# The last output tile of a transformer layer computed and stored in two column groups of 448 and 128

## Chip, cores, metric

One core of one Trainium2 chip runs the whole kernel. The metric is the device time of one execution in microseconds. It contains about 1.7 us that lie outside the profiled span (the profiled execution of the kernel before took 406.61 us with a span of 404.9).

One more length is used throughout, the **tail**: from the start of the first matmul of the last W2 tile to the end of the span. It is read from the records of a trace. The **flight** of a store is the time from the start of its issue to its landing. The **granted clock** is the share of full speed that TensorE was given.

## The reference

An attention block with a learned feature map, then a GELU MLP, both with residuals, over 2048 rows of 576 columns. Only the end matters here:

```python
def _B_ref(x, w1, b1, w2, b2):                    # D = 576, F = 4608
    y = _layernorm(x, axis=-1)
    h = _gelu(jnp.einsum("bsd,df->bsf", y, w1) + b1)
    return jnp.einsum("bsf,fd->bsd", h, w2) + b2
...
h2 = h + _B_ref(_layernorm(h, axis=-1), ...)      # 2048 x 576, bf16: the output
```

## The kernel before

The MLP runs in 8 rounds of 256 rows. Each round computes the hidden activations (W1 and GELU) and then two tiles of 128 rows x 576 output columns (W2). A tile needs 36 steps over the 4608 hidden values; the kernel lays its accumulator out in banks of 512 columns, so every step is one matmul of 512 columns and one of 64, each with its own weight load. The 64-column matmuls run five steps behind.

```python
def w2_tile(r, j, slots):
    mb = (3, 2)[j]
    for i in range(NF + LAG):                     # NF = 36, LAG = 5
        ...
        for (m, bk, o, n) in ((i, mb, 0, 512), (i - LAG, TAILB, 512, 64)):
            if 0 <= m < NF:
                P.add("pe", ... e.matmul(ps_all[:, 512*bk:512*bk + n], w2_lhs(m, j), w2_rhs(m, o, n),
                                         start=(m == 0), stop=(m == NF - 1)) ...)
    t = RT * r + j
    ob = t % 2
    P.add("pool", ... tmpo = x_all[:, t, :] + b2bc ...)          # residual + bias
    for bk, o, n in ((TAILB, 512, 64), (mb, 0, 512))[::1 - 2 * j]:
        P.add("dve", ... ostage[ob][:, o:o + n] = ps_all[bank bk] + tmpo[:, o:o + n] ...,
              writes=[res(f"ostage{ob}")] ...)
    P.dma(ch_out[ob], lambda e: e.dma_start(outr[t * 128:(t + 1) * 128, :], ostage[ob][:, :]),
          reads=[res(f"ostage{ob}")])
...
P.commit()
P.final_dma_waits("sp")     # SyncE waits for every DMA channel that it has not yet waited for
```

(`...` marks cuts; the bodies of the operations are shortened to what they compute.) `P.add` and `P.dma` record an operation; the waits between engines follow from the resources and banks that it names. A "channel" is a semaphore of its own for a row of DMAs.

The softmax here doesn't subtract the row's maximum and nothing guards it: scores larger than these inputs give would overflow.

Of the kernel before, what the change touches and what calls it, by code (L numbers as in the profile page):

```python
# [6 lines left out]
ALU = mybir.AluOpType  # L7
# [231 lines left out]
def bass_sequential_preLN__linear_kernel_hedgehog__mixer_channel_mlp__prompt_kernel(  # L239
    nc: bass.Bass,  # L240
    A_x: bass.AP,
    A_wqkv: bass.AP,
    A_w_phi: bass.AP,
    A_wo: bass.AP,
    B_x: bass.AP,
    B_w1: bass.AP,
    B_b1: bass.AP,
    B_w2: bass.AP,
    B_b2: bass.AP,
    out: bass.AP,  # L250
):
    _build(nc, A_x, A_wqkv, A_w_phi, A_wo, B_w1, B_b1, B_w2, B_b2, out)
# [48 lines left out]
def _build(nc, A_x, A_wqkv, A_w_phi, A_wo, B_w1, B_b1, B_w2, B_b2, out):  # L301
# [5 lines left out]
    NF = F // 128  # L307
    NT = S // 128
    RT = 2
    NR = NT // RT  # L310
# [6 lines left out]
    outr = out[0]  # L317

    P = Prog(nc)
# [3 lines left out]
    def sb(name, shape, dtype=BF16):  # L323
        return ctx.enter_context(nc.sbuf_tensor(name, shape, dtype))
# [4 lines left out]
    x_all = sb("x_all", [128, NT, D])  # L329
# [7 lines left out]
    ostage = [WQ[:, D * i:D * i + D] for i in range(2)]  # L337
# [32 lines left out]
    b2bc = sb("b2bc", [128, D])  # L370
# [12 lines left out]
    tmpo = sb("tmpo", [128, D], F32)  # L383
    maskf = tmpo[:, 0:133].rearrange("p (g d) -> p g d", g=7)

    ps_all = ctx.enter_context(nc.psum_tensor("ps_all", [128, 4096], F32))
    PR = 4096
    bank = [Bank() for _ in range(8)]
# [3 lines left out]
    def res(name):  # L392
        if name not in R:
            R[name] = Res(name)
        return R[name]

    def rr(fmt, n):
        return [res(fmt.format(i)) for i in range(n)]
# [6 lines left out]
          reads=[res("ident")], writes=[res("ident")])  # L405
# [3 lines left out]
          reads=[res("maskf")], writes=[res("maskf")])  # L409
    P.add("pool", lambda e: e.affine_select(maskf[:, :, :], maskf[:, :, :], pattern=[[18, 7], [0, 19]],  # L410
                                            compare_op=ALU.is_ge, fill=0.0, base=17, channel_multiplier=-1),
          reads=[res("maskf")], writes=[res("maskf")])
    P.add("pool", lambda e: e.tensor_copy(mask7[:, :, :], maskf[:, :, :]),
          reads=[res("maskf"), res("tmpo")], writes=[res("mask7")])
# [48 lines left out]
    for c in (0, 2):  # L463
# [9 lines left out]
          writes=[res("s2_0"), res("table")])  # L473
# [163 lines left out]
    for k, (b0, b1, nr) in enumerate(((0, 3, 126), (3, 4, 72), (4, 5, 126))):  # L637
# [5 lines left out]
            reads=[WPH[k], res("mask7")], writes=[res(f"phib{k}")])  # L643
# [10 lines left out]
    for g in range(4):  # L654
        n = 7 if g < 3 else 4
        P.add("pool", lambda e, g=g, n=n: e.tensor_copy(mask25[:, 7 * g:7 * g + n, :], mask7[:, 0:n, :]),
              reads=[res("mask7")], writes=[res("mask25")])
    P.add("pool", lambda e: e.tensor_copy(
        kvr[:, :, 0:25, 19:20], mask25[:, :, 0:1].unsqueeze(1).to_broadcast([128, 2, 25, 1])),
        reads=[res("mask25")], writes=[res("kvr1")])  # L660
    P.add("pool", lambda e: e.tensor_copy(
        kvr[:, :, 25:32, 19:20], mask7[:, :, 0:1].unsqueeze(1).to_broadcast([128, 2, 7, 1])),
        reads=[res("mask7")], writes=[res("kvr1")])
# [268 lines left out]
    def attn_N(t, bset):  # L932
        attn_N_mm(t, bset)
        attn_N_copy(bset, 0)
        attn_N_small(0)
        attn_N_inv(0)
        attn_N_mul(t, bset, 0, "pool")
# [11 lines left out]
    def wo_half(t, bset, step):  # L949

        A, C, B = bset
        ob = t % 2

        def one(lane, k, h, c, first, last):
            bk = (A, C)[k]
            o = 0 if c == 4 else DHF * k
            P.add(lane, lambda e: e.matmul(  # L957
                ps_all[:, 512 * bk:512 * bk + DHF], oT[ob][h:h + 64, c, :], wo_sb[h:h + 64, c, o:o + DHF],
                start=first, stop=last, skip_group_check=True),
                reads=[res(f"oT{ob}"), res("wo"), res("wo4")], banks=[bank[bk]])  # L960

        cs = (4, 0, 1, 2, 3) if step == 0 else (0, 1, 2, 3)
        lo = [lambda c=c: one("pe0", step, 0, c, c == 4, step == 1 and c == 3) for c in cs]
        hi = [lambda c=c: one("pe8", 1 - step, 64, c, c == 4, step == 1 and c == 3) for c in cs]
        return lo, hi
# [105 lines left out]
    for s in range(2):  # L1071
# [3 lines left out]
            reads=[res("mask25")], writes=[res(f"kvra{s}")], banks=[bank[5 + s]])  # L1075
# [4 lines left out]
        reads=[res("mask7")], writes=[res("kvrb")], banks=[bank[7]])  # L1080
# [4 lines left out]
    for m0 in range(0, NW2B, 8):  # L1085
# [31 lines left out]
          reads=[res("neghalf")] + rr("Eq{}", NR), writes=[res("sums0")])  # L1117
# [12 lines left out]
    TAILB = 4  # L1130
    LAG = 5
    ch_out = [P.chan(f"out{i}", "sp") for i in range(2)]
# [38 lines left out]
    def w1_round(r, extra):  # L1171

        lo, hi = [], []
        for s in range(NF // 2):
            k = s % 3
            u8 = s + (2, -1, -1)[k]
            lo += [(f, None) for f in w1_half(r, s, 0, k < 2)]
            hi += [(f, None) for f in w1_half(r, u8, 64, k == 0)]
            if k == 1:
                hi.append((None, lambda s=s: w1_act(r, s - 1)))  # L1180
            if k == 2:
                hi.append((None, lambda s=s: (w1_act(r, s), w1_act(r, s - 1))))
            for fl, fh, after in extra.get(s, ()):
                lo += [(f, None) for f in fl]
                hi += [(f, None) for f in fh]
                if after:
                    hi.append((None, after))
        hi = [(None, None)] * SKEW + hi
        n8 = 0
        while lo or n8 < len(hi):  # L1190
            if lo:
                f = lo.pop(0)[0]
                f()
            while n8 < len(hi):
                f, g = hi[n8]
                if f is None and g is not None:
                    g()
                    n8 += 1
                    continue
                if f is not None:  # L1200
                    f()
                n8 += 1
                break
            while n8 < len(hi) and hi[n8][1] is not None:
                hi[n8][1]()
                n8 += 1

    def w2_lhs(m, j):
        return hmid[:, m, 128 * j:128 * j + 128]

    def w2_rhs(m, o, n):
        return w2a[:, m, o:o + n] if m < NW2A else w2b[:, m - NW2A, o:o + n]

    def w2_tile(r, j, slots):
        mb = (3, 2)[j]
        for i in range(NF + LAG):
            if i in slots:
                slots[i]()
            for (m, bk, o, n) in ((i, mb, 0, 512), (i - LAG, TAILB, 512, 64)):
                if 0 <= m < NF:  # L1220
                    P.add("pe", lambda e, m=m, bk=bk, o=o, n=n: e.matmul(  # L1221
                        ps_all[:, 512 * bk:512 * bk + n], w2_lhs(m, j), w2_rhs(m, o, n),
                        start=(m == 0), stop=(m == NF - 1)),
                        reads=[res(f"hm{m}_{j}"), res(f"w2_{m}")], banks=[bank[bk]])
        t = RT * r + j
        ob = t % 2
        P.add("pool", lambda e: e.tensor_tensor(tmpo[:, :], x_all[:, t, :], b2bc[:, :], ALU.add),  # L1227
              reads=[res("b2"), res(f"x{t}")], writes=[res("tmpo"), res("maskf")])
        for bk, o, n in ((TAILB, 512, 64), (mb, 0, 512))[::1 - 2 * j]:
            P.add("dve", lambda e, bk=bk, o=o, n=n: e.tensor_tensor(  # L1230
                ostage[ob][:, o:o + n], ps_all[:, 512 * bk:512 * bk + n], tmpo[:, o:o + n], ALU.add),
                reads=[res("tmpo")], writes=[res(f"ostage{ob}")] + (R_weffq if t < 2 else []), banks=[bank[bk]])
        P.dma(ch_out[ob], lambda e: e.dma_start(outr[t * 128:(t + 1) * 128, :], ostage[ob][:, :]),
              reads=[res(f"ostage{ob}")])

    for r in range(NR):
        a, b = RT * (r + 1), RT * (r + 1) + 1
        extra, slots = {}, ({}, {})
        if r + 1 < NR:
            ia, ib = (3, 12) if r else (9, 16)  # L1240
            for t, i in ((a, ia), (b, ib)):
                extra[i] = [(*wo_half(t, S1, 0), None)]
                extra[i + 1] = [(*wo_half(t, S1, 1), lambda t=t: attn_wo(t, S1))]
            if r == 0:
                extra[3] = [((), (), lambda: attn_N(b, S1))]
        if r + 2 < NR:
            slots[0][2] = lambda: attn_N(a + RT, S1)
            slots[1][6] = lambda: attn_N(b + RT, S1)
        w1_round(r, extra)
        w2_tile(r, 0, slots[0])  # L1250
        w2_tile(r, 1, slots[1])

    P.commit()
    P.final_dma_waits("sp")
# [32 lines left out]
```

## Time and profile before

| | before |
|---|---|
| time, median of 3 (lowest to highest) | 406.77 us (406.11 to 407.04) |
| span of the profiled execution | 404.9 us, granted clock 1.0 |
| TensorE busy | 97% of the span |
| tail | 12.245 us: 8.98 of matmuls, 3.26 after them |

TensorE, busy for 97% of the span, bounds the kernel from beginning to end. The tail is the one place where other engines stand in the open: after the last matmul come two adds, one store and the waits for it. The prediction shows the lines. One more view, the busy time of each engine before, in and after the last tile (columns: stretch, its length, busy time and count of each engine, granted clock, DMA share, GB/s), shows the handover: 8.95 us of TensorE in 9.00, then 0.01 in 3.40.

```profile
392.60:401.60 9.00, 8.95 (x78) 4.61 (x75) 0.91 (x2) 0.00 (x0) 1.27 (x1) 1.00 0.05 16
401.60:405.00 3.40, 0.01 (x1) 0.00 (x0) 0.91 (x2) 0.00 (x0) 0.00 (x0) 1.00 0.12 43
```

### The profile page before, as it was taken

The numbers are of one execution on the slowest core, as the hardware profiler recorded it, in microseconds if no ns is written. First come the engines' busy times: TensorE is split into PE (matmuls) and PEld (weight loads), VectorE is DVE, ScalarE is ACT, GpSimd is POOL, SyncE is SP. The second block draws the span as 40 slices with busy tenths as digits, with TensorE's granted clock in tenths as the row PEclk, the third lists the DMA queues.
The fourth block names the chain that finished last, engine by engine and source line by source line (L and its number), as shares of the span: only waits on it lengthen the run. The fifth ranks groups of instructions, "written<-read, shape, count | busy, mean of one in ns | idle before, by whom it ended". The sixth has DMA issues, their size and how long they took to land.

```text
span 404.9 us, 11594 instructions
## 1 busy us (share of the span) xinstructions
PE 393.9 (97%) x4958; PEld 289.6 (72%) x4999; DVE 176.7 (44%) x415; ACT 184.8 (46%) x429; POOL 91.6 (23%) x130
## 2 busy tenths in 40 slices
PE   7899999999999999999999999999999999999996
PEld 5566666868955995599569856985797579659953
DVE  6999998876254323422442333243225402300000
ACT  6898955678820472057006600750264027404800
POOL 4759640112114002200220022002200220111000
PEclk9999999999999999999999999999999999999999
DMA  9587488981101101101111011001100110000000
GB/s 259 98 124 178 125 168 258 314 287 19 35 18 38 27 19 33 32 18 19 35 36 29 18 32 31 19 19 32 33 19 18 31 32 19 19 15 18 2 2 29
DMA packets 45594, 25.86 MB, mean 64 GB/s; under 512 B 32744, under 2 KB 44520, under 8 KB 45544
## 3 DMA queue, kind: packets, MB, share of 16 engines
q1 hardware_dynamic: 44784, 24.97, 24.5%
q8 instruction: 39, 0.64, 0.7%
q10 hardware_dynamic: 760, 0.17, 0.3%
q14 instruction: 11, 0.09, 0.1%
HBM read 15.13 MB, written 2.36 MB: 43 GB/s over the span
## 4 chain that ended last, share of the span: by engine, by line
PE 87%; ACT 6%; DVE 4%; issue 1%; DMA 1%; POOL 0%; ACTq 0%; DVEq 0%
PE ps_all L1221 34%; PE ps_all L1153 33%; PE ps_all L957 4%; PE ps_all L745 4%; PE ps_all L835 3%; PE ps_all L762 3%; PE ps_all L857 2%; PE ps_all L804 2%; ACT RA L1164 1%; ACT RB L752 1%; ACT Eq L841 1%; DMA x_all<-in_A_x_dram 1%; DVE RB L786 1%; DVE sums L773 1%; DVE x_all L979 1%
## 5 line engine op out<-in xcount | busy, mean ns | idle before, releaser
L1164 ACT ACTIVATE RA<-ps_all,b1T 128x256 bf16<-128x256 f32 x288 | 115.1, 479 | 176.6 <-PE ps_all L1153 161.9
L1153 PE MATMUL ps_all<-yT,w1sb 64*128 64x256 bf16 x2304 | 151.9, 269 | 0.0
L1153 PEld LDWEIGHTS ps_all<-yT,w1sb 64*128 64x128 bf16 x2304 | 136.2, 94 | 5.1
L1221 PE MATMUL ps_all<-w2a,RA 128*128 128x512 bf16 (+1 forms) x624 | 93.9, 284 | 2.0 <-ACT RA L1164 1.1
L1221 PEld LDWEIGHTS ps_all<-w2a,RA 128*128 128x128 bf16 x640 | 45.8, 98 | 35.7 <-ACT RA L1164 1.7
L1153 PE MATMUL ps_all<-yT,w1t 64*128 64x256 bf16 x288 | 70.9, 270 | 0.0
L1221 PE MATMUL ps_all<-RB,RA 128*128 128x512 bf16 (+1 forms) x498 | 66.6, 284 | 0.4
L1230 DVE TENSOR_TENSOR WQ<-ps_all,tmpo 128x64 bf16<-128x64 f32 (+1 forms) x32 | 14.6, 457 | 104.1 <-PE ps_all L1221 91.8
L1221 PEld LDWEIGHTS ps_all<-RB,RA 128*128 128x128 bf16 x512 | 33.4, 98 | 32.3
L979 DVE SCALAR_TENSOR_TENSOR x_all<-ps_all,x_all 128x576 bf16<-128x576 f32 x16 | 12.1, 758 | 82.8 <-PE ps_all L957 82.4
L1001 POOL TENSOR_TENSOR st<-st,neghalf 128x1 f32<-128x1 f32 x16 | 8.8, 552 | 136.3 <-DVE st L998 133.7
L925 POOL TENSOR_TENSOR obuf<-tpn 128x576 bf16<-128x576 f32 x14 | 19.6, 1400 | 84.0 <-DVE tpn L918 74.4
L841 ACT ACTIVATE Eq<-ps_all 128x512 bf16<-128x512 f32 (+1 forms) x48 | 25.1, 526 | 12.2 <-PE ps_all L835 11.3
L1227 POOL TENSOR_TENSOR tmpo<-x_all,b2bc 128x576 f32<-128x576 bf16 x16 | 20.4, 1273 | 43.2 <-DVE WQ L1230 43.2
L957 PE MATMUL ps_all<-wo_sb,OTR 64*128 64x288 bf16 x288 | 29.7, 283 | 0.5 <-ACT OTR L567 0.2
L1153 PEld LDWEIGHTS ps_all<-yT,w1t 64*128 64x128 bf16 x288 | 26.3, 94 | 1.9
L835 PE MATMUL ps_all<-yT,WQ 128*128 128x256 bf16 x200 | 25.2, 273 | 0.2 <-ACT Eq L841 0.2
L786 DVE TENSOR_TENSOR RB<-ps_all,RB 128x1152 bf16<-128x1152 f32 x16 | 21.6, 1352 | 3.4 <-PE ps_all L762 3.3
L957 PEld LDWEIGHTS ps_all<-wo_sb,OTR 64*128 64x128 bf16 x288 | 19.6, 94 | 3.8 <-PE ps_all L957 0.8
L762 PE MATMUL ps_all<-RB,yT 128*128 128x64 bf16 (+1 forms) x157 | 21.7, 284 | 0.2
L752 ACT ACTIVATE RB<-ps_all 128x576 bf16<-128x576 f32 x32 | 19.0, 648 | 5.8 <-PE ps_all L745 5.3
L745 PE MATMUL ps_all<-RA,yT 128*128 128x64 bf16 (+1 forms) x152 | 20.6, 281 | 1.1 <-ACT tpn L487 0.4
(104 smaller groups left out, 316.8 us busy)
## 6 DMA issues: line engine op xcount, KB each, us to landing
w1sb<-in_B_w_dram SPq DMA_DIRECT2D x8, 576.0 KB, 5.5
w2a<-in_B_w_dram SPq DMA_DIRECT2D x4, 720.0 KB, 7.4
RB<-in_B_w_dram SPq DMA_DIRECT2D x2, 1152.0 KB, 8.5
out_dram<-WQ SPq DMA_DIRECT2D x16, 144.0 KB, 1.8
x_all<-in_A_x_dram SPq DMA_DIRECT2D x3, 576.0 KB, 5.7
w2a<-in_A_wqkv_dram SPq DMA_DIRECT2D x2, 288.0 KB, 3.7
RB<-in_A_wqkv_dram SPq DMA_DIRECT2D x1, 576.0 KB, 5.8
w1t<-in_B_w_dram SPq DMA_DIRECT2D x2, 288.0 KB, 3.8
```

The costliest lines, as they stand in the source:

```text
L745: P.add("pe", lambda e, c=c, o=o, n=n: e.matmul(ps_all[:, 512 * KB + o:512 * KB + o + n], yT[:, c, sl * 128:(sl + 1) * 128], weffk[:, c, o ...
L752: P.add("act", lambda e, s=s: e.activation(Ek[eb][:, D * s:D * s + D], ps_all[:, 512 * KB:512 * KB + D], AF.Exp, scale=1.0 if s == 0 else ...
L762: P.add("pe", lambda e, c=c, o=o, n=n: e.matmul(ps_all[:, 512 * VB + o:512 * VB + o + n], yT[:, c, sl * 128:(sl + 1) * 128], wv[:, c, o:o ...
L786: P.add("dve", lambda e, s0=s0, s1=s1: e.tensor_tensor(vx(t)[:, s0:s1, :, 0:DH], ps_all[:, 512 * VB:512 * VB + D].rearrange("p (h d) -> p ...
L835: P.add("pe", lambda e, i=i, c=c, h0=h0: e.matmul(ps_all[:, 512 * bk + RW * i:512 * bk + RW * i + RW], weffq[:, c, DH * h0:DH * h0 + 128], ...
L841: P.add("act", lambda e, s=s: e.activation(Eq[:, r, s, bs[0]:bs[0] + n, :], ps_all[:, 512 * bk:512 * bk + RW * n].rearrange("p (b t) -> p ...
L925: P.add(oeng, lambda e: e.tensor_tensor(obuf[ob][:, 0:D], tpn[:, 0, :], tpn[:, 1, :], ALU.add), reads=[res("tpn")], writes=[res(f"obuf{ob}")])
L957: P.add(lane, lambda e: e.matmul(ps_all[:, 512 * bk:512 * bk + DHF], oT[ob][h:h + 64, c, :], wo_sb[h:h + 64, c, o:o + DHF], start=first, s ...
L1153: P.add(lane, lambda e: e.matmul(ps_all[:, o:o + RW], lhs, yT[h:h + 64, c, ys], start=first, stop=not begin and i == 1 and c == 3, skip_gr ...
L1164: P.add("act", lambda e, m=m, o=o: e.activation(hmid[:, m, :], ps_all[:, o:o + RW], AF.Gelu_apprx_tanh, bias=b1T[:, m:m + 1]), reads=[res( ...
L1221: P.add("pe", lambda e, m=m, bk=bk, o=o, n=n: e.matmul(ps_all[:, 512 * bk:512 * bk + n], w2_lhs(m, j), w2_rhs(m, o, n), start=(m == 0), st ...
L1227: P.add("pool", lambda e: e.tensor_tensor(tmpo[:, :], x_all[:, t, :], b2bc[:, :], ALU.add), reads=[res("b2"), res(f"x{t}")], writes=[res(" ...
```

## The change

The intent is to have most of the last tile summed, added and on its way to memory while TensorE still works on the rest. Only the 16th tile is touched: its 576 columns are split 448 + 128, each group runs through all 36 steps by itself, then is added, then stored: the first on output channel 0, the second on channel 1, the two that the earlier tiles use in turn.

```diff
+    def w2_last(r, j):
+        t, ob = RT * r + j, (RT * r + j) % 2
+        P.add("pool", lambda e: e.tensor_tensor(tmpo[:, :], x_all[:, t, :], b2bc[:, :], ALU.add), ...)
+        for k, (bk, o, n) in enumerate(((2, 0, 448), (TAILB, 448, 128))):
+            for m in range(NF):
+                P.add("pe", lambda e, m=m, bk=bk, o=o, n=n: e.matmul(
+                    ps_all[:, 512 * bk:512 * bk + n], w2_lhs(m, j), w2_rhs(m, o, n),
+                    start=(m == 0), stop=(m == NF - 1)), ...)
+            P.add("dve", lambda e, bk=bk, o=o, n=n: e.tensor_tensor(
+                ostage[ob][:, o:o + n], ps_all[:, 512 * bk:512 * bk + n], tmpo[:, o:o + n], ALU.add),
+                reads=[res("tmpo")], writes=[res(f"ostage{ob}{k}")] + ..., banks=[bank[bk]])
+            P.dma(ch_out[k], lambda e, o=o, n=n: e.dma_start(
+                outr[t * 128:(t + 1) * 128, o:o + n], ostage[ob][:, o:o + n]), reads=[res(f"ostage{ob}{k}")])
...
-        w2_tile(r, 1, slots[1])
+        if r + 1 < NR:
+            w2_tile(r, 1, slots[1])
+        else:
+            w2_last(r, 1)
```

More of the change, by code (lines that the diff above doesn't have):

```diff
@@ L1212, in w2_rhs @@
         return w2a[:, m, o:o + n] if m < NW2A else w2b[:, m - NW2A, o:o + n]
+    def w2_last(r, j):
+        t, ob = RT * r + j, (RT * r + j) % 2
+        P.add("pool", lambda e: e.tensor_tensor(tmpo[:, :], x_all[:, t, :], b2bc[:, :], ALU.add),
+              reads=[res("b2"), res(f"x{t}")], writes=[res("tmpo"), res("maskf")])
+        for k, (bk, o, n) in enumerate(((2, 0, 448), (TAILB, 448, 128))):
+            for m in range(NF):
+                P.add("pe", lambda e, m=m, bk=bk, o=o, n=n: e.matmul(
+                    ps_all[:, 512 * bk:512 * bk + n], w2_lhs(m, j), w2_rhs(m, o, n),
+                    start=(m == 0), stop=(m == NF - 1)),
+                    reads=[res(f"hm{m}_{j}"), res(f"w2_{m}")], banks=[bank[bk]])
+            P.add("dve", lambda e, bk=bk, o=o, n=n: e.tensor_tensor(
+                ostage[ob][:, o:o + n], ps_all[:, 512 * bk:512 * bk + n], tmpo[:, o:o + n], ALU.add),
+                reads=[res("tmpo")], writes=[res(f"ostage{ob}{k}")] + ([res(f"ostage{ob}")] if k == 0 else []), banks=[bank[bk]])
+            P.dma(ch_out[k], lambda e, o=o, n=n: e.dma_start(
+                outr[t * 128:(t + 1) * 128, o:o + n], ostage[ob][:, o:o + n]), reads=[res(f"ostage{ob}{k}")])
     def w2_tile(r, j, slots):
```

## The prediction

> **What bounds the kernel now.** I read the first page for the engine that is always busy, then the chain of work that ended last over the last 22 us, then the timeline of the last tile instruction by instruction, and last the queue of the sync engine, which issues the store and waits for it. On the page:
>
> ```profile
> PE 393.9 (97%) x4958; PEld 289.6 (72%) x4999; DVE 176.7 (44%) x415; ACT 184.8 (46%) x429; POOL 91.6 (23%) x130
> PE 87%; ACT 6%; DVE 4%; issue 1%; DMA 1%; POOL 0%; ACTq 0%; DVEq 0%
> ```
>
> TensorE is the bound from end to end, so a change in one tile of 16 can matter in two ways only: through the time that the tile keeps TensorE, and through what follows the last matmul, when nothing else is left to overlap. The diff touches nothing before the last W2 tile. The chain, at its end:
>
> ```profile
> 396.87 4.76 PE ps_all L1221 x42
> 401.63 0.00 issue
> 401.63 0.70 DVE WQ L1230
> 402.33 0.02 issue
> 402.35 0.22 DVE WQ L1230
> ```
>
> TensorE leads up to 401.63 us; then VectorE adds 512 columns (0.69 us) and 64 columns (0.22 us) one after the other, both in the open. What follows is the store: timeline, then the DMA view of the last 3 us, then the sync engine's waits.
>
> ```profile
> 402.65 0.33 SPq L1233 DMA_DIRECT2D out_dram<-WQ  x1
> ...
> out_dram<-WQ SPq DMA_DIRECT2D x1, 144.0 KB, 1.7
> ...
> SPq L226 <- DMA out_dram<-WQ: 0.2, 1, 0.2
> ```
>
> The store is issued at 402.65, lands 1.74 us later at 404.39 (both from the trace's record of this one DMA), and the program ends at 404.87. The third line is easy to pass over: of that flight SyncE waits only 0.2 us. The records of its queue say why. After issuing the store it works through some twenty waits for every earlier load, each about 60 ns apart, from 403.03 to 404.22, and only then comes to the store's own. So a store that lands faster gains at most about 0.17 us; from there the list is the bound.
>
> How the last tile feeds TensorE, from the timeline of that tile:
>
> ```profile
> 397.38 0.38 PE L1221 MATMUL ps_all<-RB,RA 128*128 128x512 bf16 x1
> 397.60 0.19 PE L1221 MATMUL ps_all<-w2a,RA 128*128 128x64 bf16 x1
> 397.63 0.38 PE L1221 MATMUL ps_all<-RB,RA 128*128 128x512 bf16 x1
> 397.85 0.19 PE L1221 MATMUL ps_all<-w2a,RA 128*128 128x64 bf16 x1
> 397.87 0.38 PE L1221 MATMUL ps_all<-RB,RA 128*128 128x512 bf16 x1
> ```
>
> Read the starts, not the durations, which overlap: 512 columns take 0.216 us and 64 take 0.029, 0.245 a pair, although each has its own weight load. The lag of five leaves five 64-column matmuls alone at the end (starts 401.303 to 401.420 us in the records, 29 ns apart, one bank), so repeated accumulation into one bank costs nothing extra, and a load can hide behind as little as 29 ns.
>
> [...] the trace of before does not bear it out. Its 128-column matmuls with a weight load each are the transposes (first line below), whose starts in the records are 56 ns apart (88.302, 88.358, 88.414, 88.470); and a group of eight 133-column and two 76-column matmuls (second line) takes 0.72 us in all[...].
>
> ```profile
> 88.30 0.39 PE L563 MATMUL ps_all<-ident,ybuf 128*128 128x128 bf16 x4
> 44.66 0.72 PE L804 MATMUL ps_all<-RB 128*128 128x133 bf16 x10
> ```
>
> [...] the two forms here show 691 and 224:
>
> ```profile
> L1230 DVE TENSOR_TENSOR WQ<-ps_all,tmpo 128x512 bf16<-128x512 f32 x16 | 11.1, 691 | 40.1 <-PE ps_all L1221 39.8
> L1230 DVE TENSOR_TENSOR WQ<-ps_all,tmpo 128x64 bf16<-128x64 f32 x16 | 3.6, 224 | 64.0 <-PE ps_all L1221 51.9 <-issue 8.6 <-POOL tmpo L1227 3.2
> ```
>
> [...] The new last store has rows of 256 bytes (128 columns of bf16), the old one 1152. No store of before is that narrow, so no line here shows its price. [...] of 1.74 us, the packets run from 403.48 to 404.01 only; 0.83 us pass before them and 0.38 after.
>
> **The change part by part.**
> Removed: the lagged pairing in tile 15 (36 matmuls of 512 and 36 of 64 columns), the adds of 512 and 64, one store of 144 KB. Added: 36 matmuls of 448, then 36 of 128, adds of 448 and 128, stores of 112 KB and 32 KB on the two output channels. The comparison of the queues shows no other difference: one more DMA on SyncE, equal counts on ACT and DVE, the same 72 matmuls. GpSimd's add of residual and bias waits for the same adds as before and is done some 6 us before it is needed (from 394.01 for 1.27 us).
> TensorE: before 36 x (215.8 + 29.2) = 8.82 us. [...] The same 576 columns a weight, the same 72 fixed costs: zero.
> The first group ends about 392.63 + 6.81 = 399.44. Its add (448 columns: 624 ns) and its store (issue 0.33, landing 1.7) are over by about 402.2, the issue by 400.9: all beside the second group's 2.01 us of matmuls or before the second store needs the queue.
> Last matmul: it starts at 392.63 + 8.82 - 0.06 = 401.39; a 128-column matmul lasts 219 ns by the transposes, so 401.61.
> Add of 128 columns: [...] It waits for one semaphore only; VectorE operations of this sort (the copies after the kv matmuls) start 37 ns after the matmul's modelled end. The old first add started 190 ns after its own last matmul, with two more waits of 50 ns ahead of it; those waits now stand before the 448-column add, out of sight. So 401.65 to 401.94, against 402.58 before: 0.64 us gained. It is 0.69 + 0.03 + 0.22 = 0.94 taken away and 0.29 put back, less 0.02 because the old add, freed by the 512-column group before the last 64-column matmuls were through, began 17 ns after TensorE's last end and the new one begins 37 ns after it.
> Store: issued 75 ns after the add as before, at 402.02. Its packets are 256 bytes: before, each engine ran eight rows 47 ns apart, 0.38 us. If a short row takes a third of that, landing comes 0.25 us earlier, 1.5 us after issue, at about 403.5. But the list of waits ends 1.62 us after the issue, at 403.64, against the old landing-bound check at 404.41. Gain at the end: 0.77 us. If the short rows save nothing, it is 0.64.
> I choose 0.72, between the two and nearer the list.
>
> **The rivals.**
> (a) Weight loads bind at 128 columns: [...] Against it: the 56 ns of the transposes and the 29 ns at the end of this very tile. I give it one in twenty.
> (b) The narrow store is slow. [...] Against it: there is only 32 KB, and most of the flight is before and after the packets. One in six.
> (c) The end is hidden anyway, behind the list of waits. It takes away at most the 0.1 us by which landing would beat it; it cannot take the 0.64, because the list starts with the issue of the last store and moves with it.
> (d) Run noise. Three runs of before span 0.93 us, more than the whole gain.
>
> **Range and chances.** The profiled execution of before took 406.61 with a span of 404.9, so about 1.7 us lie outside the span and do not move. 406.77 - 0.72 = 406.05. The median of before stands a little above the middle of its own runs, so I round down to 406.0. The range takes (b) at one end and a luckier set of runs at the other: 405.4 to 406.6. Two per cent is 8.1 us; nothing in the last tile (about 9 us of matmuls, 3 us of tail) could move that much: within 2% at 0.99.
>
> **What would show it.** Right: in the last 12 us the 128-column matmuls start 56 ns apart; the add of 128 columns takes 0.29 us and is the only VectorE piece of the chain after the last matmul; the 448-column add lies inside the matmuls; the last store issues at about 402.0, and the span is near 404.15. SyncE's wait for the last store should shrink from 0.2 us to almost nothing. Wrong: [...] landing over 1.8 us after issue (b); the 448-column add or its store delaying the second; or anything changed before 392 us, which the diff gives no reason for.

Passages that no trace or run of this case shows are cut from the prediction, and the cuts are marked. The sum stays as it was: 0.77 us gained at the end, 0.64 if the short rows save nothing, 0.72 chosen, 406.77 - 0.72 = 406.05, rounded down to 406.0. Terms are cut out of it: the matmuls of the two groups (6.81 and 2.01 us, together the 8.82 of before, hence zero for TensorE) and the working of the 128-column add (0.29 us). For these and for the 624 ns of the 448-column add an estimate from the trace of before gives the same: a straight line through its matmuls of 64 and 512 columns (29.2 and 215.8 ns) passes 55.9 at 128, with the transposes at 56 beside it, and 189.1 at 448, and leaves 2.5 ns at no columns (the "fixed cost" of each), and one through its adds of 64 and 512 columns (224 and 691 ns) passes 291 at 128 and 624 at 448. The "it" that the trace does not bear out is rival (a), a slower run of loads and matmuls. Of the group of ten matmuls only the reading is left: in the records the next matmul starts 0.560 us after the first of the ten, 1216 columns at 2.17 a ns. Rival (b) supposed, with nothing here to show it, that a narrow row takes twice the 47 ns: 0.38 us more, a gain of about 0.26, 406.5.

## The result

| | before | after |
|---|---|---|
| median of 4 runs (lowest to highest) | 406.9 us (406.11 to 407.19) | 406.0 us (405.57 to 406.78) |
| ratio, 95% interval | | 0.9983 [0.9962, 1.0004] |
| the same in a later, longer comparison (10 runs, 6 runs) | 407.0 us | 406.21 us, 0.9981 [0.9968, 0.9994] |
| tail, first trace / repeats | 12.245 / 12.249 us | 11.452 / 11.451, 11.448 us |

A ratio is the mean time of one kernel's fast runs over that of the other's of the same rounds, so not quite the ratio of the medians. By the first comparison alone the change could be nothing; the second leaves 1 outside its interval; the tails settle it: 0.80 us, repeated to 5 ns.

The chain of work that ended last, after (start, length, what; the columns of the chain in the prediction). The adds of 0.70 + 0.02 + 0.22 us at the end have become one of 0.29:

```profile
383.63 8.93 PE ps_all L1237 x72
392.56 8.84 PE ps_all L1220 x72
401.39 0.02 issue
401.42 0.29 DVE WQ L1224
```

TensorE and VectorE in the timeline after. The 448-column add (0.62 us) starts at 399.56, under the 128-column matmuls; twenty of these start at 399.20 and the next group of sixteen at 400.32, 56 ns for each:

```profile
399.20 1.28 PE L1220 MATMUL ps_all<-w2a,RA 128*128 128x128 bf16 x20
399.56 0.62 DVE L1224 TENSOR_TENSOR WQ<-ps_all,tmpo 128x448 bf16<-128x448 f32 x1 [5.86 <-PE ps_all L1220]
...
400.32 1.06 PE L1220 MATMUL ps_all<-RB,RA 128*128 128x128 bf16 x16
401.42 0.29 DVE L1224 TENSOR_TENSOR WQ<-ps_all,tmpo 128x128 bf16<-128x128 f32 x1 [1.23 <-PE ps_all L1220]
```

The stores after (bytes, median us from issue to landing), and what SyncE's queue waited for from 399 us on (total, times, longest):

```profile
out_dram<-WQ SPq DMA_DIRECT2D x1, 112.0 KB, 1.7
out_dram<-WQ SPq DMA_DIRECT2D x1, 32.0 KB, 1.5
...
SPq L226 <- DVE WQ L1224: 7.2, 2, 6.1
SPq L1275 <- PEq L1275: 0.2, 1, 0.2
```

The last of these lines belongs to the program's own end. The line "SPq L226 <- DMA out_dram<-WQ", 0.2 us before, is gone: when SyncE comes to its last wait, at 403.38 us, the store has landed (403.26). What ends last is now its list of waits. An absent line is as much a reading as a present one.

### The profile page after: what moved, and what is told of

Its sections match the earlier page's. It is cut to its first block, busy times and chain, and to the rows that moved or that the text cites. A ratio compares the mean times of both kernels' runs of the same rounds, so it can differ in the third digit from the quotient of the medians.

```text
span 403.8 us, 11636 instructions
## 1 busy us (share of the span) xinstructions
PE 396.6 (98%) x4999; PEld 289.8 (72%) x4999; DVE 176.8 (44%) x415; ACT 184.4 (46%) x429; POOL 91.5 (23%) x130
## 4 chain that ended last, share of the span: by engine, by line
PE 90%; DVE 5%; DMA 2%; ACT 1%; issue 1%; POOL 0%; DVEq 0%; ACTq 0%
PE ps_all L1153 35%; PE ps_all L1237 33%; PE ps_all L957 5%; PE ps_all L745 4%; PE ps_all L762 4%; PE ps_all L835 3%; PE ps_all L857 2%; PE ps_all L1220 2%; PE ps_all L804 2%; DMA yT<-ybuf 1%; DVE bns L494 1%; DMA x_all<-in_A_x_dram 1%; DVE sums L773 1%; DVE ybuf L526 1%; DVE x_all L979 1%
## 5 line engine op out<-in xcount | busy, mean ns | idle before, releaser
L1237 PE MATMUL ps_all<-w2a,RA 128*128 128x64 bf16 (+1 forms) x600 | 90.3, 286 | 0.0
L1237 PEld LDWEIGHTS ps_all<-w2a,RA 128*128 128x128 bf16 x600 | 42.9, 98 | 33.4 <-ACT RA L1164 1.7
L1237 PE MATMUL ps_all<-RB,RA 128*128 128x64 bf16 (+1 forms) x480 | 63.4, 286 | 0.0
L1246 DVE TENSOR_TENSOR WQ<-ps_all,tmpo 128x64 bf16<-128x64 f32 (+1 forms) x30 | 13.7, 458 | 96.3 <-PE ps_all L1237 84.0
L1237 PEld LDWEIGHTS ps_all<-RB,RA 128*128 128x128 bf16 x480 | 31.4, 98 | 30.3
L1243 POOL TENSOR_TENSOR tmpo<-x_all,b2bc 128x576 f32<-128x576 bf16 x15 | 19.1, 1272 | 17.4 <-DVE WQ L1246 17.4
L745 PE MATMUL ps_all<-RA,yT 128*128 128x512 bf16 (+1 forms) x160 | 22.4, 286 | 0.3 <-DMA yT<-ybuf 0.2
L762 PE MATMUL ps_all<-RB,yT 128*128 128x512 bf16 (+1 forms) x160 | 22.2, 286 | 0.0
```

The costliest lines, as they stand in the source:

```text
L745: P.add("pe", lambda e, c=c, o=o, n=n: e.matmul(ps_all[:, 512 * KB + o:512 * KB + o + n], yT[:, c, sl * 128:(sl + 1) * 128], weffk[:, c, o ...
L762: P.add("pe", lambda e, c=c, o=o, n=n: e.matmul(ps_all[:, 512 * VB + o:512 * VB + o + n], yT[:, c, sl * 128:(sl + 1) * 128], wv[:, c, o:o ...
L1237: P.add("pe", lambda e, m=m, bk=bk, o=o, n=n: e.matmul(ps_all[:, 512 * bk:512 * bk + n], w2_lhs(m, j), w2_rhs(m, o, n), start=(m == 0), st ...
L1243: P.add("pool", lambda e: e.tensor_tensor(tmpo[:, :], x_all[:, t, :], b2bc[:, :], ALU.add), reads=[res("b2"), res(f"x{t}")], writes=[res(" ...
```

## The experiments

All tails, in us from the first matmul of the last tile, from the records of each trace. Every kernel below computes the right result; single times are of unknown state and are not used.

| run | last matmul ends | last add ends | last store issued | landed | end (tail) |
|---|---|---|---|---|---|
| before | 8.98 | 9.95 | 10.02 | 11.77 | 12.245 |
| r_before | 8.98 | 9.95 | 10.03 | 11.77 | 12.249 |
| after | 8.98 | 9.31 | 9.39 | 10.86 | 11.452 |
| r_after, t_after | 8.98 | 9.31 | 9.39 | 10.86 | 11.451, 11.448 |
| e_one_store | 8.98 | 9.31 | 9.39 | 11.13 | 11.612 |
| e_two_stores | 8.98 | 9.82 | 10.19 | 11.70 | 12.307 |
| e_rev | 8.98 | 9.65 | 9.72 | 11.39 | 11.876 |
| e_512_64 | 8.98 | 9.25 | 9.32 | 10.81 | 11.430 |
| e_hoist | 8.98 | 9.31 | 9.39 | 10.87 | 11.347 |
| e_before_hoist | 8.98 | 9.95 | 10.04 | 11.78 | 12.255 |
| e_fresh | 8.98 | 9.31 | 9.34 | 10.80 | 11.455 |
| e_best | 8.98 | 9.25 | 9.29 | 10.82 | 11.307 |
| e_480_96 | 8.98 | 9.28 | 9.31 | 10.75 | 11.236 |

The first column is the same in every row: however the 576 columns are cut or ordered, 72 matmuls with 72 weight loads take the same time. No part of any difference comes from TensorE.

**Does the tail repeat?** No edit, both kernels profiled again.

> The kernel before, unchanged, profiled a second time, to see how well the length of the tail repeats. Tail = from the first matmul of the last W2 tile to the end of the span. First trace: 404.87 - 392.63 = 12.25 us. If the tail is set by a fixed chain of instructions, as my theory says, it repeats within 0.05 us, while the time of the tile's start moves by some tenths from execution to execution. If the gain were mere run noise (rival), the tail itself would move by some tenths too.

> The changed kernel, unchanged, profiled a second time. First trace: tail 403.85 - 392.39 = 11.46 us. Theory: 11.46 again within 0.05, so that the change is worth 0.79 us whatever the start of the tile. Noise rival: the tail moves by some tenths.

Tails of 12.249 and 11.451 us. The start of the last tile moved meanwhile: 392.63 and 392.39 us in the two traces of before, 392.39, 392.94 and 392.69 in three of after. So the scatter of the times is made upstream of the change, and noise explains none of the 0.80 us.

**The column groups without the split store.**

```diff
-            P.dma(ch_out[k], ... outr[t * 128:(t + 1) * 128, o:o + n], ostage[ob][:, o:o + n]), ...)
+        P.dma(ch_out[ob], ... outr[t * 128:(t + 1) * 128, :], ostage[ob][:, :],
+              reads=[res(f"ostage{ob}{k}") for k in range(2)])
```

> The column groups and the two adds stay, but tile 15 is stored by one DMA of 144 KB after the second add. Theory (the gain is the add of 512 columns moved beside the matmuls, 0.64 us, plus up to 0.15 us from the smaller store): the store is issued as in the changed kernel, 9.39 us after the tile's start, lands 1.74 us later and the end is landing-bound 0.48 us after that: tail 11.61. Rival (most of the gain comes from the small last store landing sooner): tail back near 12.2.

11.612 us. The adds' share of the gain is 12.245 - 11.612 = 0.63 us; the smaller last store gives the other 0.16. The flight is 1.741 us, as before, and SyncE waits for it again, which the line absent above now shows:

```profile
SPq L226 <- DVE WQ L1224: 7.6, 1, 7.6
SPq L226 <- DMA out_dram<-WQ: 0.2, 1, 0.2
```

**The split store without the column groups.**

```diff
-        for k, (bk, o, n) in enumerate(((2, 0, 448), (TAILB, 448, 128))):
-            for m in range(NF): ...matmuls of this group...
+        for i in range(NF + LAG):
+            for (m, bk, o, n) in ((i, 2, 0, 512), (i - LAG, TAILB, 512, 64)): ...matmul if 0 <= m < NF...
+        for k, (bk, o, n) in enumerate(((2, 0, 512), (TAILB, 512, 64))):
```

> The matmuls interleaved in pairs of 512 and 64 columns as before, adds of 512 and 64 as before, but each stored by itself. Theory: both adds still stand in the open and the second store has to queue behind the issue of the first (0.33 us), so its issue slips from 10.02 to about 10.18 us after the tile's start, and the faster landing only pays this back: the list of waits ends 2.06 us before the end as in the changed kernel, tail about 12.24, no gain. Rival (the split of the store is what pays): tail near 11.6 to 12.0.

12.307 us: no gain, and 0.06 worse than before (I had 0.00). In the timeline the two adds now take 0.82 us where before they took 0.95: they name different resources, so the second no longer waits for VectorE's semaphore as it does before, and it started 85 ns before the first one's end. That 0.13 us was an unplanned help, and it was lost again: the second store waited for the first one's issue, came 0.37 us after its add in place of 0.07, and its own issue took 0.384 us in place of 0.332.

```profile
401.89 0.82 DVE L1226 TENSOR_TENSOR WQ<-ps_all,tmpo 128x512 bf16<-128x512 f32 x2 [7.70 <-PE ps_all L1221]
...
402.66 0.81 SPq L1229 DMA_DIRECT2D out_dram<-WQ  x2
```

**The groups in the other order.**

```diff
-        for k, (bk, o, n) in enumerate(((2, 0, 448), (TAILB, 448, 128))):
+        for k, (bk, o, n) in enumerate(((2, 448, 128), (TAILB, 0, 448))):
```

> The same two groups in the other order: 128 columns first, 448 last. Theory: the add of 448 columns (0.625 us) now stands in the open instead of 128 (0.292), and the last store has 896-byte rows that land in 1.69 us, so the end is landing-bound: last matmul ends 8.98 us after the tile's start, add to 9.64, issue 9.72, landing 11.41, end 11.89. So it keeps about 0.35 of the 0.79 us. Rival (having two groups is enough, whichever is last): tail 11.46.

11.876 us, 0.01 from the sum. It is the size of the last group that counts, not that there are two: the add left in the open took 0.624 us in place of 0.292, and the flight 1.671 in place of 1.475.

**Where the list of waits stands.** The waits for the loads move ahead of the first of the two last stores; in the control, ahead of the single last store of the kernel before.

```diff
+    def early_waits():
+        P.commit()
+        for pid, ch in P.chans.items():
+            if pid not in ch_out and ch["count"] > P.seen["sp"].get(pid, 0):
+                op = _Op(None)
+                op.waits.append((pid, ch["count"]))
+                P.ops["sp"].append(op)
+                P.seen["sp"][pid] = ch["count"]
...
+            if k == 0:
+                early_waits()
             P.dma(ch_out[k], ...)
```

> The changed kernel, but SyncE's waits for all the earlier loads are put before the first of the two last stores, where SyncE has nothing to do, so that after the last store only the waits for the stores are left. Theory (the list of waits is what ends last in the changed kernel): the end becomes landing-bound, issue 9.39 + 1.475 + 0.485 = 11.35, a gain of 0.11 over 11.46. Rival (the end is landing-bound already): 11.46, no change.

> The control: the same move of the waits in the kernel before. There the store lands 0.18 us after the list is through, so theory says no gain: tail 12.25 within 0.05. If the list of waits were a cost in itself there too (rival), it would gain some tenths.

11.347 us, 0.105 less, with everything up to the landing unchanged; and 12.255 us in the control, no gain. So the list is what ends last after the change, and hides behind the store before it. (This execution of e_hoist reached the last tile at 394.74 us, some 2 us later than the others; the matmuls of the tile took the same 8.98 us.) In e_hoist the wait for the stores is back, and long, because nothing stands in front of it:

```profile
SPq L226 <- DVE WQ L1233: 5.7, 2, 4.6
SPq L226 <- DMA out_dram<-WQ: 1.1, 1, 1.1
```

**A narrower last group.**

```diff
-        for k, (bk, o, n) in enumerate(((2, 0, 448), (TAILB, 448, 128))):
+        for k, (bk, o, n) in enumerate(((2, 0, 512), (TAILB, 512, 64))):
```

> Groups of 512 and 64 columns. The last group's matmuls need 36 x 29 ns = 1.05 us, just enough to cover the first add (0.19 us to start, 0.69 long). Theory: the last add takes 0.224 instead of 0.292 us, all else is bound by the list of waits: tail 11.39. The store has rows of 128 bytes; if narrow rows cost time (rival), its landing would be later than the 1.475 us of the 256-byte store; I expect 1.45. A second rival, that weight loads bind a run of 36 matmuls of 64 columns, would show as starts more than 29 ns apart.

11.430 us: 0.022 of the 0.067 expected. The add took 0.225 as foreseen and the matmuls start 29 ns apart. But the second store followed on the first one's heels (issues at 401.804 and 402.233), its own issue took 0.377 us, and the list behind it began that much later. The flight was 1.491 us, not shorter than the 1.475 of rows twice as wide; but it counts from the start of the longer issue, and from the end of the issue the narrow store landed after 1.114 us, the wider one after 1.143. I had not thought of stores hindering each other.

**A channel of its own for the last store.**

```diff
-    ch_out = [P.chan(f"out{i}", "sp") for i in range(2)]
+    ch_out = [P.chan(f"out{i}", "sp") for i in range(3)]
-            P.dma(ch_out[k], ...)
+            P.dma(ch_out[2 * k], ...)
```

> The changed kernel with a channel of its own (its own semaphore) for the last store, so that its issue waits for the add only and not also for the last store but two on the same channel. Theory: one wait instruction between the add and the issue less, so the issue comes 30 to 45 ns after the add in place of 74, and the whole list with it: tail about 11.42. Rival: the wait costs nothing, tail 11.46.

A miss: 11.455 us, no gain. The issue did come sooner, 27 ns after the add in place of 74. But the third channel adds one more wait to the list, and this list is what ends last: from the issue to its last wait it took 1.645 us in place of 1.596. The step can pay only where the list is out of the way.

**The three together, and the changed kernel beside it.**

> All three together: groups of 512 and 64, waits for the loads moved ahead, a channel of its own for the last store. Theory, adding the steps: last matmul ends 8.99 us after the tile's start, add to 9.25, issue 9.29, landing 1.45 later, end 0.485 after that: tail 11.22, that is 1.03 us under the kernel before and 0.24 under the changed one; time about 405.7 beside 406.8 of before, if the runs' scatter lets it be seen. If the gains do not add (rival: some other wait holds the end), the tail stays near 11.35.

> The changed kernel in five rounds on the same chip as the previous one. Theory: 0.8 us under before, ratio 0.998; the interval may still reach 1, as the runs of one kernel scatter over 0.9 us. Tail of the trace 11.46.

11.307 us, not 11.22, and 405.83 us (median of 5), ratio 0.9974 [0.9961, 0.9987]; the changed kernel beside it 406.21 us, ratio 0.9981 [0.9968, 0.9994]. The missing 0.09 us lie in the flight, 1.529 us instead of 1.45: the issue started at 9.294 us, as expected, 51 ns after the end of the first one's issue, but took 0.424 us.

**The same with room between the stores.**

```diff
-        for k, (bk, o, n) in enumerate(((2, 0, 512), (TAILB, 512, 64))):
+        for k, (bk, o, n) in enumerate(((2, 0, 480), (TAILB, 480, 96))):
```

> As e_best, but with groups of 480 and 96 columns. In e_best the second store came within 0.05 us of the end of the first one's issue; its own issue took 0.424 instead of 0.332 us and its flight 1.53 instead of the 1.46 of the 256-byte store in e_fresh. Theory (two stores issued close together hinder one another): with 96 columns the last group takes 36 x 42.5 ns = 1.53 us, the first store is through its issue some 0.6 us before the second, which then issues in 0.332 and lands in 1.46: last matmul ends about 8.98 us after the tile's start, [...] issue 9.30, landing 10.76, end 11.25 against 11.31 of e_best. Rival (it is the narrowness of the rows or of the last store that slowed e_best): issue and flight as slow as there or in between, tail 11.31 to 11.35.

The 42.5 ns for 96 columns are an estimate, the middle between the 29.2 and 55.8 ns of 64 and 128 columns (before, after). The cut term put the end of the add at 9.28 us; the middle between the adds of 64 and 128 columns (0.224 and 0.292 us) gives the same, and the add took 0.26 us.

11.236 us, issue 0.332 and flight 1.444 us. Rows of 192 bytes with room flew faster than rows of 256 (1.460 in e_fresh) and of 128 without room (1.529), so the rival of rows that slow down step by step with their width falls.

This edit changed the width and the distance together, though, and no run has rows of 128 bytes with room. The traces kept of the three runs with 128-byte rows separate the two: the second issue started 93, 97 and 51 ns after the end of the first (e_two_stores, e_512_64, e_best) and took 0.384, 0.377 and 0.424 us, so it ended 0.474 to 0.477 us after the first's end every time. A cost of the width alone would not depend on the distance. Loads in the trace of before show the same least spacing: three of them, issued 42 to 43 ns behind another, ended 0.474 to 0.477 us after it, and none ended sooner. And counted from the end of the issue all these stores landed alike, 1.105 to 1.126 us with rows of 128 bytes, 1.112 with 192, 1.127 and 1.143 with 256 (e_fresh, after): the longer flights are the longer issues.

The time is 405.49 us (405.31 to 405.57, 4 runs), ratio 0.9962 [0.9947, 0.9977]: the lowest median and the shortest tail. The tail accounts for 1.01 us; the medians lie 1.7 us apart (407.2 of before). Where the rest comes from is not shown: the runs of before scatter (406.41 to 408.7), and ten of these eleven are those of the comparison above, only the slowest is new. SyncE's queue, e_best first, then e_480_96: two issues that fill 0.81 us without a gap worth naming, and two over 1.24 us, with SyncE waiting 0.6 us for the add in between.

```profile
401.68 0.81 SPq L1238 DMA_DIRECT2D out_dram<-WQ  x2
```

```profile
400.85 1.24 SPq L1238 DMA_DIRECT2D out_dram<-WQ  x2
...
SPq L1238 <- DVE WQ L1233: 0.6, 1, 0.6
```

## Why the prediction was right

The time (406.0 us predicted, 406.0 measured) fits better than it deserves: a median of four runs that span 1.2 us can't be foreseen to 0.1. The steps can be judged by the tail, where 0.77 was the sum, 0.72 the choice, and 0.79 to 0.80 came out.

- *TensorE: zero.* Right. Its last matmul ends 8.98 us into the tile in all kernels, and the 128-column matmuls start 56 ns apart.
- *Rival (a), weight loads bind at 128 columns.* Fell: 56 ns at 128 columns, and 29 at 64 in e_512_64.
- *The first group's add and store lie beside the second group's matmuls.* Right: add 399.56 to 400.19, store issued by 400.59, both before the last matmul.
- *The last add: 0.29 us, starting 37 ns after the last matmul.* 0.292 us, 38 ns. The 0.64 us predicted for this part are the 0.63 of e_one_store.
- *The store lands earlier, 1.5 us after issue.* 1.475. A row of 256 bytes took 15 to 18 ns in place of about 51 for 1152. Rival (b), that a narrow row takes twice the time, fell; per byte it was slower, as 14.5 bytes moved in a ns in place of 22.6.
- *The list of waits then binds, so that landing earlier gains at most some 0.15.* Right, and shown twice: by the missing wait line, and by e_hoist, which took out the 0.105 us between landing and list and nothing else. The list came to its last wait 1.596 us after the issue instead of the 1.62 I had worked out, which is the 0.02 us by which 0.77 was short. My choice of 0.72 leaned the wrong way from it.
- *The span near 404.15.* 403.85, because that execution reached the tile 0.24 us earlier than the trace of before. Another trace of before did the same: scatter, not the change.

## What to carry to other kernels

When one engine is busy to the end, look at what follows its last instruction, and cut the last piece of work so that only a small piece stands there; the cut costs nothing where the engine's time goes by columns, as it did here for groups of 64 to 512 (29 ns a matmul at 64, 56 at 128, 189 at 448, 216 at 512; the last one ended 8.98 us into the tile in every run). Then find which of the waits at the end comes last: here it was the store before the change, the program's own list of old waits after it, and, in the first attempt to go further, a store issued too closely behind another. A change of under a microsecond in 400 is judged by the length of the tail in the trace, not by the time.

## What the runs measured of the hardware

- Matmuls in a row, each with its own weight load, started 216 ns apart at 512 columns and 29 at 64 (before), 189 at 448 and 56 at 128 (after).
- Packets of 1152 bytes took 51 ns on average (before), of 256 bytes 17.6 (after) and of 128 bytes 12.5 (e_best), that is 22.6, 14.5 and 10.2 bytes per ns; why a narrow row moves fewer bytes in a ns no run shows. For one small store this weighs little: the packets of the 32 KB store ran for 0.26 us of its flight of 1.475, and stores with rows of 256 bytes flew 1.46 to 1.50 us in all runs, with 192 bytes 1.44, against 1.74 for the store of 144 KB.
- Where a store was issued right behind another from the same queue, the second issue ended no sooner than 0.474 us after the end of the first, and so took 0.377, 0.384 and 0.424 us in place of 0.332 (e_512_64, e_two_stores, e_best). The mechanism stays open: no run here tells one cause from another.
- A wait that was already satisfied took about 60 ns for each instruction of SyncE's list, 1.2 us for twenty of them (before, 403.03 to 404.22 us), and the list became the bound of the end.
